# Second block scheme in a fused attention and tanh-shrink kernel: two groups of the first matrix, thirteen normalizations on ScalarE, one shared store of buffers

## The chip, the cores and the metric

The kernel runs on one core of one Trainium2 chip. The metric is the device time of one execution in microseconds, as the median of several runs. A profiled execution also gives a trace: what every engine did and when. The engines are TensorE (PE, with its weight loads as PEld), VectorE (DVE), ScalarE (ACT), GpSimd (POOL) and SyncE (SP); POOL, SP and ACT also issue DMAs from queues of their own, in order.

## The reference

Attention over 4 batches, 8 heads, 768 positions and 64 dimensions, where each query sees 96 local keys and 8 global ones, and then an MLP over the 3072 tokens of 512 features:

```python
scores = scale * np.matmul(q, k.transpose(0, 1, 3, 2)) + bias   # bias: -slope * distance
scores = np.where(is_global | is_local, scores, -1e9)
a = softmax(scores)
x = (a @ v) as 3072 x 512
h = x @ w_in            # 512 x 2048
g = h - np.tanh(h)
out = g @ w_out         # 2048 x 512
```

## The kernel before

**Tiles.** The 3072 tokens are 24 tiles of 128, numbered in the order in which they are worked on. Attention goes tile by tile: transposes of q and k (T, by PE for the first tiles and by DMA from SP's queue afterwards), scores on PE (S, line 375), exp on ACT (E, line 382), the mask as a product on DVE (M, line 386), the product with v on PE (AV, line 401; v has a column of ones, which yields the sum), and the normalization on DVE (R, lines 409 and 410: a reciprocal of 8 numbers a row, and a product that writes x, 512 columns). The 8 global rows of k and v are copied into each tile's own buffers (K and V, DVE copies). Then x is transposed (X and Xe for the first eight tiles, a DMA on SP's queue afterwards, Xe, line 432).

**First matrix.** Tiles are put in groups: groups 0 and 1 have one tile, 2 to 6 have two, 7 to 9 have four. W_in's 2048 columns are 16 blocks f of 128. For groups of four tiles an operation m1.g.f is four matmuls (line 443) of 128 x 128 weights over 512 columns (tokens) into one PSUM bank; th.g.f is the tanh on ACT from that bank (line 453), and g.g.f the subtraction on DVE (line 467), which writes g in bf16.

**Second matrix.** Each pair of tiles a, a+1 is multiplied with W_out by a block scheme with seven products instead of eight (Strassen's, in a form with intermediate sums): n1 to n4 are sums of blocks of g on DVE (line 507), w1 to w4 sums of blocks of W_out (line 494, once), p1 to p7 the products on PE (line 522), each of eight matmuls of 256 columns with its own weights. Some products accumulate onto one bank one after another, and what stands there is copied out between them (a0, a1, a2: 256 columns to SBUF, ACT or DVE, lines 253 and 255). c11, c12, c21 and c22 make the four blocks of the result (line 536 and the copy helper), and st stores 128 rows (line 539) from POOL's or SP's queue. For the last pair p3 and c12 are cut in halves.

**Order.** The list ORDER gives the order of issue on all engines at once, one word for each operation: `m1.8.11` is group 8, block 11; a side after a slash (`a1.14/a`) names the engine where there is a choice (a ACT, d DVE, p POOL, s SP). Each engine works through its own words in this order and waits only for what it needs. The list HOMES names the buffer or bank that each holder uses. Both lists are written out; the rest of the code only says what each word does. Buffers of three kinds (kq natural q and k, qk transposed q and k, pr exponentials) are separate sets of 5, 11 and 5 buffers, 2 KB a partition each.

Of the kernel before, what the change touches and what calls it, by code (L numbers as in the profile page):

```python
# [20 lines left out]
lq.4 Te.2.0/a AV.1 E.0.0 S.2 R.1 in.2 B.3 E.2.0 lk.4 AV.0 S.3 R.0 X.1 in.4 E.3.0 AV.2 Xe.1/d X.0 in.5 R.2 bm.2 Xe.0/a  # L21
AV.3 m1.1.0 lk.5 em.2 R.3 X.2 m1.0.0 th.1.0 Xe.2/d X.3 lq.5 th.0.0 g.1.0 m1.0.2 Xe.3/a g.0.0 m1.1.2 th.0.2 m1.2.2 th.1.2
g.0.2 g.1.2 lv.4 m1.2.6 th.2.2 lk.6 g.2.2 T.4.0 th.2.6 m1.2.0 Te.4.0/a m1.1.4 lq.6 th.2.0 m1.0.4 lv.5 th.1.4 g.1.4 T.4.1
m1.2.4 Te.4.1/a g.2.0 th.0.4 S.4 th.2.4 g.0.4 out.0 m1.2.10 E.4.0 K.4 g.2.6 m1.1.8 E.4.1 M.4.0 m1.2.8 g.2.4 th.1.8 out.1
M.4.1 th.2.10 m1.2.12 th.2.8 g.1.8 out.2 T.5.1 g.2.10 th.2.12 T.5.0 m1.1.12 out.3 Te.5.1/d Te.5.0/a g.2.12 S.5 lk.7
th.1.12 g.2.8 AV.4 g.1.12 E.5.1 lq.7 m1.0.8 R.4 E.5.0 m1.0.12 lq.10 M.5.1 M.5.0 T.6.1 lq.9 th.0.12 X.4 T.6.0 V.4 Xe.4/a
K.5 n1.0 AV.5 Te.6.1/a m1.2.14 R.5 th.0.8 Te.6.0/a lk.10 X.5 th.2.14 S.6 Xe.5/d g.0.12 m1.3.4 E.6.1 g.0.8 m1.3.6 g.2.14
lq.8 w1.0 m1.3.10 th.3.6 n3.0 th.3.4 m1.3.8 n2.0 E.6.0 w1.1 m1.3.12 th.3.10 g.3.6 lk.8 p1.0 g.3.4 m1.3.0 n1.2 a0.0/a
th.3.8 w3.0 m1.3.2 th.3.0 w2.0 lk.9 p2.0 w2.1 lv.6 w3.1 p6.0 g.3.0 T.7 lv.7 p7.0 n3.2 a1.0/a th.3.2 w4.0 p5.0 th.3.12
g.3.2 n2.2 a2.0/a p1.2 g.3.10 p2.2 a0.2/a c22.0 w4.1 p6.2 n4.2 T.8 p4.0 c11.0 a1.2/a g.3.12 p5.2 c21.0 T.9 M.6.1  # L30
st.1.0/p p7.2 a2.2/a c11.2 lv.8 g.3.8 T.10 p3.2 K.6 lq.13 V.5 M.6.0 S.7 c12.2/a c22.2 lq.11 AV.6 n4.0 E.7.1 p4.2 lk.12
R.6 E.7.0 m1.3.14 st.2.0/p M.7.1 lv.10 K.7 X.6 V.6 th.3.14 M.7.0 p3.0 Xe.6/a lv.9 c21.2 AV.7 g.3.14 c12.0/a lk.11 R.7
S.8 lq.12 n1.4 X.7 E.8.0 p1.4 Xe.7/d V.7 n2.4 m1.4.8 E.8.1 M.8.0 lk.13 m1.4.10 a0.4/a K.9 M.8.1 th.4.8 lk.15 p6.4 g.4.8
th.4.10 lv.11 E.9.0 g.4.10 m1.4.14 a1.4/d S.9 th.4.14 g.4.14 p5.4 E.10.1 K.10 M.9.0 m1.4.0 E.9.1 n3.4 T.11 AV.8 M.10.1
th.4.0 m1.4.4 a2.4/d E.10.0 T.12 R.8 p7.4 th.4.4 g.4.0 st.3.0/s m1.4.6 M.9.1 Xe.8 g.4.4 p2.4 th.4.6 c22.4 T.13 AV.9 n4.4
m1.4.12 R.9 m1.4.2 g.4.6 Xe.9 p3.4 c11.4 th.4.2 M.10.0 th.4.12 p4.4 g.4.2 c12.4/a g.4.12 st.4.0/p S.10 V.9 lq.14 n1.6
p1.6 E.11.1 c21.4 lq.15 n2.6 p2.6 E.11.0 a0.6/d lk.14 K.11 AV.10 c11.6 E.12.0 lv.12 p6.6 K.12 R.10 lq.16 m1.5.10 V.10
a1.6/a M.11.0 lk.16 S.11 th.5.10 lv.13 g.5.10 p5.6 E.12.1 M.11.1 m1.5.8 E.13.0 n4.6 T.14 AV.11 n3.6 th.5.8 m1.5.2 R.11
E.13.1 T.15 m1.5.12 g.5.8 th.5.2 M.12.1 m1.5.14 Xe.11 th.5.12 V.11 a2.6/a M.12.0 m1.5.0 M.13.0 Xe.10 AV.12 g.5.2 th.5.0
m1.5.6 th.5.14 R.12 T.16 p7.6 th.5.6 V.12 g.5.12 p3.6 Xe.12 c22.6 g.5.6 m1.5.4 c12.6/a g.5.14 st.6.0/p g.5.0 p4.6 th.5.4  # L40
lv.14 g.5.4 S.12 lv.15 M.13.1 p1.8 E.14.0 c21.6 st.5.0/p K.15 n1.8 m1.6.4 lk.18 E.15.0 K.14 a0.8/d AV.13 n2.8 lk.17
# [36 lines left out]
p.6.0:2 s.6.1:2,3 p.6.1:1 av.6:0,1 xt.6:7 x.6:0 s.7.0:4,5 p.7.0:1 s.7.1:6,7 p.7.1:3 av.7:4,5 xt.7:4 x.7:0 s.8.0:0,1
p.8.0:1 s.8.1:2,3 p.8.1:3 av.8:6,7 x.8:0 s.9.0:6,7 p.9.0:2 s.9.1:0,1 p.9.1:4 av.9:2,3 x.9:2 s.10.0:2,3 p.10.0:1
# [36 lines left out]
def kernel(  # L116
# [50 lines left out]
    u = 0  # L167
# [530 lines left out]
```

## Time and profile before

| | us |
|---|---|
| median of 3 runs | 204.03 (204.01 to 205.84) |
| the profiled execution | 203.72 |
| its span, first to last instruction | 202.0 |
| PE busy, 2147 matmuls | 194.3 |
| DVE busy, 360 instructions | 169.1 |
| ACT busy, 199 instructions | 120.0 |
| POOL busy, 102 instructions | 77.8 |

The span is what the trace covers; the execution's own time holds some 1.7 us more around it. In a row of instructions of the trace stand the start, the time, the engine, the line of the code, the operation, what it writes and reads with its shape, how many of them in a row, and in brackets how long the engine was idle before and which instruction ended that. A group's row ends with the total, the mean of one in ns, and the idle time of the engine before such instructions. Rows of one line give least, median and most of the duration in ns. Issues of DMAs are listed with their size and the median time from issue to landing.

### The profile page before, as it was taken

The page shows a single profiled execution, that of the slowest core. Times are in us where ns is not written, and L with a number is a line of the kernel's source. Part 1 is how long each engine was busy: PE and PEld are TensorE (multiplying, and loading weights), DVE is VectorE, ACT ScalarE, POOL GpSimd, SP SyncE. Part 2 cuts the span into 40 slices and gives each one's busy share as a digit, 9 for nine tenths or more (in the row PEclk, how much of TensorE's full clock was granted, in tenths as well). Part 3 has the DMA queues.
Part 4 walks back from the last instruction along what each step waited for, and adds up shares of the span by engine and source line. Part 5 has one row for each costly group of instructions (what it writes and reads, how often), then busy time and mean ns, then how long its engine had stood idle before and what let it go on. Part 6 is the DMA issues. An engine that isn't in the chain of part 4 may idle for free.

```text
span 202.0 us, 5299 instructions
## 1 busy us (share of the span) xinstructions
PE 194.3 (96%) x2147; PEld 149.8 (74%) x2147; DVE 169.1 (84%) x360; ACT 120.0 (59%) x199; POOL 77.8 (39%) x102
## 2 busy tenths in 40 slices
PE   7799999999999999999999999999999999999991
PEld 2469888888888988888988654787655456778890
DVE  6685798999998998999999799899896799659731
ACT  3798888652679287756746866686345563542120
POOL 8986485351981066069129900404001000001212
PEclk9999999999999999999999999999999999999999
DMA  5999999999999989979979999899250201002133
GB/s 142 218 184 184 194 167 207 198 154 151 204 172 156 206 132 134 167 159 169 142 155 160 185 127 167 161 92 148 67 130 0 104 3 52 0 0 109 52 124 136
DMA packets 103175, 27.33 MB, mean 135 GB/s; under 512 B 93920, under 2 KB 101344, under 8 KB 103152
## 3 DMA queue, kind: packets, MB, share of 16 engines
q0 software_dynamic: 74400, 17.90, 89.7%
q1 hardware_dynamic: 28208, 8.59, 25.2%
q10 hardware_dynamic: 544, 0.52, 1.0%
q8 instruction: 16, 0.26, 0.5%
q14 instruction: 7, 0.06, 0.1%
HBM read 27.26 MB, written 6.29 MB: 166 GB/s over the span
## 4 chain that ended last, share of the span: by engine, by line
PE 54%; issue 15%; DMA 12%; POOL 8%; DVE 8%; POOLq 0%
PE ps L443 28%; PE ps L522 19%; DMA w_out_bf<-in_moe_w_out_dram 6%; DMA w_in_bf<-in_moe_w_in_dram 6%; PE ps L401 4%; PE ps L375 4%; POOL w_in_bf L324 2%; POOL vb L321 2%; DVE gall L467 2%; POOL out_dram L539 2%; POOL kq L318 1%; DVE wc L494 1%; DVE pr L386 1%; DVE ot L536 1%; POOL kq L321 1%
## 5 line engine op out<-in xcount | busy, mean ns | idle before, releaser
L443 PE MATMUL ps<-xT,w_in_bf 128*128 128x256 bf16 (+2 forms) x640 | 91.1, 294 | 0.0
L467 DVE TENSOR_TENSOR gall<-ps,th 128x512 bf16<-128x512 f32 (+1 forms) x98 | 63.0, 673 | 14.9 <-ACT th L453 14.4
L453 ACT ACTIVATE th<-ps 128x512 f32<-128x512 f32 (+1 forms) x98 | 55.4, 591 | 32.6 <-PE ps L443 30.2
L443 PEld LDWEIGHTS <-w_in_bf 128*128 128x128 bf16 x640 | 56.4, 98 | 22.6
L522 PEld LDWEIGHTS <-gall 128*128 128x128 bf16 x488 | 46.6, 98 | 8.1 <-issue 0.5
L539 POOL DMA_DIRECT2D out_dram<-ot x19 | 10.8, 567 | 106.4 <-ACT ot L253 40.3
L382 ACT ACTIVATE pr<-ps 128x1024 bf16<-128x1024 f32 x44 | 43.5, 1025 | 6.2 <-PE ps L375 3.6
L522 PE MATMUL ps<-w_out_bf,gall 128*128 128x256 bf16 (+1 forms) x296 | 36.7, 270 | 0.4 <-DVE ot L255 0.4
L386 DVE TENSOR_TENSOR pr<-pr,mk 128x1024 bf16<-128x1024 bf16 x40 | 26.7, 680 | 0.6 <-ACT pr L382 0.5
L253 ACT COPY sn<-ps 128x256 f32<-128x256 f32 x29 | 10.8, 371 | 27.1 <-PE ps L522 27.0
L522 PE MATMUL ps<-f,ss 128*128 128x256 bf16 x192 | 24.9, 273 | 0.0
L522 PE MATMUL ps<-wc,gall 128*128 128x256 bf16 x192 | 24.9, 273 | 0.0
L321 POOL DMA_DIRECT2D vb<-in_v_dram x24 | 21.5, 906 | 1.2 <-DMA w_in_bf<-in_moe_w_in_dram 0.7
L321 POOL DMA_DIRECT2D kq<-in_k_dram x20 | 18.1, 912 | 6.3 <-DMA w_out_bf<-in_moe_w_out_dram 4.4
L522 PEld LDWEIGHTS <-ss 128*128 128x128 bf16 x192 | 18.1, 98 | 2.9
L536 DVE TENSOR_TENSOR ot<-ps,sn 128x256 f32<-128x256 f32 x36 | 14.8, 418 | 5.6 <-PE ps L522 4.3
L321 POOL DMA_DIRECT2D kq<-in_q_dram x20 | 18.0, 911 | 3.4 <-DMA w_out_bf<-in_moe_w_out_dram 2.0
L410 DVE TENSOR_TENSOR x<-ps,rden 128x512 bf16<-128x512 f32 x24 | 16.6, 692 | 1.1 <-DVE rden L409 0.3
L401 PEld LDWEIGHTS <-pr 128*128 128x128 bf16 x352 | 13.4, 97 | 2.6 <-ACT pr L382 0.5
L401 PE MATMUL ps<-vb,pr 128*128 128x65 bf16 x352 | 14.8, 193 | 0.0
L375 PEld LDWEIGHTS <-qk 64*128 64x128 bf16 x352 | 10.0, 94 | 3.5 <-issue 2.7
L375 PE MATMUL ps<-qk 64*128 64x128 bf16 x192 | 9.4, 218 | 0.0
(57 smaller groups left out, 122.9 us busy)
## 6 DMA issues: line engine op xcount, KB each, us to landing
out_dram<-ot POOLq DMA_DIRECT2D x18, 256.0 KB, 2.5
vb<-in_v_dram POOLq DMA_DIRECT2D x24, 128.0 KB, 5.8
kq<-in_q_dram POOLq DMA_DIRECT2D x22, 128.0 KB, 6.8
kq<-in_k_dram POOLq DMA_DIRECT2D x22, 128.0 KB, 6.7
w_out_bf<-in_moe_w_out_dram POOLq DMA_DIRECT2D x4, 512.0 KB, 10.8
out_dram<-ot SPq DMA_DIRECT2D x5, 256.0 KB, 2.5
w_in_bf<-in_moe_w_in_dram POOLq DMA_DIRECT2D x4, 256.0 KB, 7.4
w_in_bf<-in_moe_w_in_dram POOLq DMA_DIRECT2D x2, 512.0 KB, 11.2
```

The costliest lines, as they stand in the source:

```text
L321: eng(e).dma_start(out=dst, in_=rows_of(src, u).rearrange("h p d -> p h d"))
L375: nc.tensor.matmul(bank(("s", u, o), hh)[:, p * P : (p + 1) * P], buf(("qk", back[u] if o else u))[r, 1, p, :], buf(("qk", u))[r, 0, p, :] ...
L382: nc.scalar.activation(d, banks(("s", u, o), 0, 1), AF.Exp, bias=0.0, scale=scale)
L386: nc.vector.tensor_tensor(out=t, in0=t, in1=mk[:, mask_of(u, o)], op=ALU.mult)
L401: nc.tensor.matmul(t[:, h // (H // 2), h % (H // 2), :], buf(("p", u, o))[:, slot(h), :], buf(("v", back[u] if o else u))[:, h, 0 : Dh + 1 ...
L410: nc.vector.tensor_tensor(out=buf(("x", u)).rearrange("q (a h) d -> q a h d", a=2), in0=t[:, :, :, 0:Dh], in1=rden.to_broadcast([P, 2, H / ...
L443: nc.tensor.matmul(t[:, (f - f0) * n : (f - f0 + 1) * n], w_in_bf[j][:, c, fo : fo + P], x[:, c, 0:n], start=(c == 0), stop=(c == CD - 1),)
L453: nc.scalar.activation(h_view(buf(("th", g, f0)), g, m), h_view(bank(("h", g, f0)), g, m), AF.Tanh, bias=0.0, scale=1.0)
L467: nc.vector.tensor_tensor(out=o, in0=v(h), in1=v(th), op=ALU.subtract)
L522: nc.tensor.matmul(bank((holder, a))[:, c0:c1], s(f), t(f)[:, c0:c1], start=first and f == 0, stop=f == HF - 1, skip_group_check=not first,)
L536: nc.vector.tensor_tensor(out=o, in0=bank((holder, a))[:, 0:DH2], in1=buf(("sn", a, k)), op=ALU.add)
L539: eng(e).dma_start(out=out[turn_of[u] * P : (turn_of[u] + 1) * P, c0:c1], in_=buf(("ot", u))[:, c0:c1])
```

## The change

**The first matrix of groups 8 and 9 by a block scheme.** W_in's 16 blocks of columns are four runs of four blocks. For runs j = 1, 2, 3 of groups 8 and 9 (six units g.j) the sixteen m1 matmuls of 512 columns are replaced by seven products d1 to d7, each of four matmuls of 256 columns (two blocks of outputs r, two of the contraction c). Run 0 keeps m1. A unit has three banks: r and q (side by side in the code as `qr`) and z. d1 starts r, and e0 copies its 512 columns to SBUF in fp32 (k0); d6 accumulates onto r, e1 copies; d5 accumulates, e2 copies; d3 accumulates, and r then holds one block of h. d2 goes to q, and q11 (DVE) adds k0 to it. d7 goes to z, q22 adds it to e2's copy; d4 accumulates onto z, q21 adds it to e1's copy. The tanh and the subtraction are as many as before, 512 columns each, but read their h from two banks or two SBUF buffers. y1 to y4 are four sums of x blocks for each of the two groups, v1 to v4 four sums of W_in blocks for each of the three runs, on DVE, 512 bf16 columns each.

```diff
+    DUNITS = [(8, 1), (8, 2), (8, 3), (9, 1), (9, 2), (9, 3)]
...
+    def wi_sum(j, k):
+        a, b = 4 * j, 4 * j + 2
+        x, y, o = {
+            1: (w_in_two(b, 0), w_in_two(b, 2), ALU.add), 2: (wsum(j, 1), w_in_two(a, 0), ALU.subtract),
+            3: (w_in_two(a, 0), w_in_two(b, 0), ALU.subtract), 4: (w_in_two(a, 2), wsum(j, 2), ALU.subtract),
+        }[k]
+        nc.vector.tensor_tensor(out=wsum(j, k), in0=x, in1=y, op=o)
+
+    def x_sum(g, k):
+        b11, b12, b21, b22 = (x_block(g, i, j) for i in (1, 2) for j in (1, 2))
+        x, y = {1: (b12, b11), 2: (b22, xsum(g, 1)), 3: (b22, b12), 4: (b21, xsum(g, 2))}[k]
+        nc.vector.tensor_tensor(out=xsum(g, k), in0=x, in1=y, op=ALU.subtract)
...
+    def in_product(g, j, k):
+        a, b = 4 * j, 4 * j + 2
+        part, w, x, first = {
+            1: ("r", lambda r: w_in_of(a + r, 0), x_block(g, 1, 1), True),
+            2: ("q", lambda r: w_in_of(a + r, 2), x_block(g, 2, 1), True),
+            3: ("r", lambda r: wsum(j, 4)[:, :, r * P : (r + 1) * P], x_block(g, 2, 2), False),
+            4: ("z", lambda r: w_in_of(b + r, 2), xsum(g, 4), False),
+            5: ("r", lambda r: wsum(j, 1)[:, :, r * P : (r + 1) * P], xsum(g, 1), False),
+            6: ("r", lambda r: wsum(j, 2)[:, :, r * P : (r + 1) * P], xsum(g, 2), False),
+            7: ("z", lambda r: wsum(j, 3)[:, :, r * P : (r + 1) * P], xsum(g, 3), True),
+        }[k]
+        t = d_bank(g, j, part)
+        for r in range(2):
+            for c in range(2):
+                nc.tensor.matmul(
+                    t[:, r * 2 * P : (r + 1) * 2 * P], w(r)[:, c], x[:, c], start=first and r + c == 0, stop=c == 1,
+                    skip_group_check=not first or r > 0,
+                )
+
+    def d_copy(e, g, j, k):
+        copy(e, d_keep(g, j, k), d_bank(g, j, "r"))
+
+    def d_add(g, j, k):
+        if k == 0:
+            q = d_bank(g, j, "q")
+            nc.vector.tensor_tensor(out=q, in0=q, in1=d_keep(g, j, 0), op=ALU.add)
+            return
+        a = d_keep(g, j, k)
+        nc.vector.tensor_tensor(out=a, in0=d_bank(g, j, "z"), in1=a, op=ALU.add)
```

**Normalization.** R keeps only the reciprocal; the product is a word of its own, N, with a choice of engine. Eleven tiles have it on DVE as before (N/d), thirteen on ACT (N/a: 4, 8, 9, 11 to 15, 17, 20 to 23), where it is eight activations of 64 columns, one a head, whose scale is a column of the reciprocals.

```diff
+    def a_N(e, u):
+        t, rden = av(u), rdens[home(("rd", u))[0]]
+        if e is ACT:
+            for h in range(H):
+                a, b = divmod(h, H // 2)
+                nc.scalar.activation(
+                    buf(("x", u))[:, h, :], t[:, a, b, 0:Dh], AF.Copy, bias=0.0, scale=rden[:, a, b, :]
+                )
+            return
```

**K and V.** They get a choice of engine: 8 of 16 K and 7 of 16 V go to ACT.

**One store.** The 21 buffers of kq, qk and pr become slots of one tile `mem` of the same total size; the new sums and copies (ws, xs, k0, k12: one or two slots each) take slots of it too, and HOMES says who has which.

```diff
-    buffers("kq", NK, [P, 2, H * Dh], BF16)
-    buffers("qk", NQK, [P, 2, NP, P], BF16)
+    mem = pool.tile([P, NM, 2 * H * Dh], BF16, name="mem")
...
-    buffers("pr", 5, [P, H, P], BF16)
```

**Order and homes.** Both lists are new from the normalization of the first tiles on. Stores go from SP's queue twelve times instead of seven and from POOL's fourteen instead of nineteen. The new list where the block products are, and its end:

```diff
+p3.12 M.22.0 E.22.1 S.18 c22.12 M.21.0 c12.12/a p4.12 E.23.0 M.20.1 st.12.0/p p1.14 M.21.1 lv.23 E.23.1 M.23.0 AV.20
+st.11.0/p y1.8 d1.8.1 V.20/a y2.8 d2.8.1 R.20 e0.8.1/a y4.8 AV.21 N.20/a c21.12 d6.8.1 M.22.1 m1.8.0 a0.14/a R.21 Xe.20
+q11.8.1 e1.8.1/a p2.14 N.21/a n3.14 V.21/d d5.8.1 c11.14 th.8.0 Xe.21 d1.8.3 y3.8 e2.8.1/a g.8.0 AV.22 e0.8.3/a d3.8.1
+R.22 M.23.1 d7.8.1 N.22/a p6.14 V.22/d q22.8.1 th.8.5 Xe.22 d1.8.2 n4.14 th.8.4 d4.8.1 e0.8.2/a g.8.5 d6.8.3 q21.8.1
+d2.8.2 e1.8.3/a d6.8.2 g.8.4 th.8.6 d5.8.3 q11.8.2 e1.8.2/a AV.23 e2.8.3/a g.8.6 d7.8.3 a1.14/a d2.8.3 R.23 th.8.7
+q22.8.3 d5.8.2 N.23/a d3.8.3 q11.8.3 d4.8.3 g.8.7 e2.8.2/a Xe.23 d7.8.2 th.8.13 q21.8.3 d3.8.2 th.8.12 p5.14 q22.8.2
...
+p5.18 g.9.11 th.9.1 c21.16 p7.18 g.9.6 a2.18/a st.17.0/s th.9.10 g.9.0 p3.16 g.9.1 p3.18 g.9.10 c22.18 p1.20 n1.20 p2.20
...
+st.22.0/p p5.22 p3.20 a2.22/d c22.22 p3.22.0 c11.20 c12.20/a p4.22 st.20.0/s c12.22.0/a st.22.256/p p3.22.1 c21.22
+c12.22.1/a st.23.0/s st.22.384/s
```

More of the change, by code (lines that the diff above doesn't have):

```diff
@@ L25 @@
[L25 to L29, printed above, removed]
@@ new lines @@
+q21.8.2 d1.9.1 g.8.15 th.8.10 d2.9.1 g.8.14 e0.9.1/a m1.8.2 th.8.11 g.8.1 th.8.3 m1.9.3 y2.9 a2.14/a q11.9.1 p3.14
+g.8.10 th.9.3 g.8.3 d6.9.1 th.8.2 m1.9.2 g.8.11 e1.9.1/a c12.14/a y3.9 d5.9.1 g.9.3 th.9.2 st.14.0/p d1.9.2 e2.9.1/a
+y4.9 d2.9.2 g.8.2 e0.9.2/a d7.9.1 c22.14 d3.9.1 q22.9.1 d6.9.2 th.9.5 n1.16 p1.16 th.9.4 g.9.5 e1.9.2/a p4.14 q11.9.2
+a0.16/a d4.9.1 g.9.4 d5.9.2 q21.9.1 d1.9.3 e2.9.2/a n3.16 d2.9.3 e0.9.3/a d7.9.2 c21.14 n2.16 d3.9.2 st.15.0/s d6.9.3
+n1.18 p6.16 e1.9.3/a q22.9.2 d5.9.3 n3.18 a1.16/a d7.9.3 e2.9.3/a g.9.2 d4.9.2 th.9.9 p5.16 q22.9.3 th.9.7 q11.9.3
@@ L112 @@
+ot.16:2 ot.17:2 r.18:5 q.18:7 z.18:3 sn.18.0:2 sn.18.1:1 sn.18.2:0 ss.18.1:2 ss.18.2:1 ot.18:3 ot.19:0 r.20:2 q.20:4
+z.20:7 sn.20.0:0 sn.20.1:2 sn.20.2:1 ss.20.1:2 ss.20.2:1 ot.20:0 ot.21:1 r.22:3 q.22:5 z.22:7 sn.22.0:1 sn.22.1:3
+sn.22.2:1 ss.22.1:0 ss.22.2:3 ot.22:3 ot.23:1 g.0:0 g.2:1 g.4:2 g.6:0 g.8:2 g.10:0 g.12:1 g.14:2 g.16:0 g.18:1 g.20:3
+g.22:4 mk.1:2,3 mk.2:0,1 f32.0.k:3 f32.0.q:2 f32.1.k:1 f32.1.q:0
 """
@@ L221, in home, with mems @@
         return homes[".".join(map(str, holder))]
-    KIND = {"v": "vb", "p": "pr"}
-    def buf(holder):
+    KIND = {"v": "vb"}
+    def mems(holder, dt):
+        i, j = home(holder)
+        t = mem[:, i : j + 1, :].rearrange("q a f -> q (a f)")
+        return t if dt is BF16 else t.bitcast(dt)
+    def buf(holder):
+        k = holder[0]
+        if k in ("kq", "qk", "p", "k0"):
+            t = mem[:, home(holder)[0], :]
+            if k == "kq":
+                return t.rearrange("q (a f) -> q a f", a=2)
+            if k == "qk":
+                return t.rearrange("q (a p f) -> q a p f", a=2, p=NP)
+            return t.rearrange("q (h f) -> q h f", h=H) if k == "p" else t.bitcast(FP32)
         return bufs[KIND.get(holder[0], holder[0])][home(holder)[0]]
@@ L446, in m1, with w_in_of, w_in_two, four @@
                 )
+    def w_in_of(f, c):
+        j = in_of[f]
+        return w_in_bf[j][:, c : c + 2, (f - in_from[j]) * P : (f - in_from[j] + 1) * P]
+    def w_in_two(f, c):
+        j = in_of[f]
+        fo = (f - in_from[j]) * P
+        return w_in_bf[j][:, c : c + 2, fo : fo + 2 * P]
+    def four(holder):
+        return mems(holder, BF16).rearrange("q (k c f) -> q k c f", k=4, c=2)
+    def wsum(j, k):
+        return four(("ws", j))[:, k - 1]
+    def xsum(g, k):
+        return four(("xs", g))[:, k - 1]
@@ new lines, in d_bank, with d_keep @@
+    def d_bank(g, j, part):
+        return bank(("zd", g, j)) if part == "z" else bank(("qr", g, j), 0 if part == "q" else 1)
+    def d_keep(g, j, k):
+        return buf(("k0", g, j)) if k == 0 else mems(("k12", g, j), FP32)[:, (k - 1) * 4 * P : k * 4 * P]
+    def in_product(g, j, k):
[16 more added lines that the diff above has]
+                )
@@ L448, in h_view, with d_th, d_g @@
+    def d_th(g, f):
+        o = buf(("th", g, f)).rearrange("q (b n) -> q b n", b=2)
+        nc.scalar.activation(o, h_of(g, f), AF.Tanh, bias=0.0, scale=1.0)
+    def d_g(g, f):
+        us = groups[g]
+        i, j = home(pair_of(us[0]))[0], home(pair_of(us[2]))[0]
+        th = buf(("th", g, f)).rearrange("q (b n) -> q b n", b=2)
+        nc.vector.tensor_tensor(out=gall[:, i : j + 1 : j - i, f, :], in0=h_of(g, f), in1=th, op=ALU.subtract)
     def h_view(t, g, m):
@@ L598 @@
         if 1 <= nth[u] < NQ - 1:
-            op(("K", u), DVE, lambda e, u=u: a_K(e, u))
-            op(("V", u), DVE, lambda e, u=u: a_V(e, u))
+            op(("K", u), None, lambda e, u=u: a_K(e, u))
+            op(("V", u), None, lambda e, u=u: a_V(e, u))
         op(("AV", u), PE, lambda e, u=u: a_AV(u))
         op(("R", u), DVE, lambda e, u=u: a_R(u))
+        op(("N", u), None, lambda e, u=u: a_N(e, u))
         if u < PE_X:
@@ L613 @@
         for f, m in ([(0, 2), (2, 2)] if m == 4 else []) + [(f, m) for f in range(4 if m == 4 else 0, CF, m)]:
+            if (g, f // 4) in DUNITS:
+                op(("th", g, f), ACT, lambda e, g=g, f=f: d_th(g, f))
+                op(("g", g, f), DVE, lambda e, g=g, f=f: d_g(g, f))
+                continue
             op(("m1", g, f), PE, lambda e, g=g, f=f, m=m: m1(g, f, m))
@@ L616 @@
             op(("g", g, f), DVE, lambda e, g=g, f=f, m=m: m1_g(g, f, m))
+    for j in sorted({j for _, j in DUNITS}):
+        for k in range(1, 5):
+            op((f"v{k}", j), DVE, lambda e, j=j, k=k: wi_sum(j, k))
+    for g in sorted({g for g, _ in DUNITS}):
+        for k in range(1, 5):
+            op((f"y{k}", g), DVE, lambda e, g=g, k=k: x_sum(g, k))
+    for g, j in DUNITS:
+        for k in range(1, 8):
+            op((f"d{k}", g, j), PE, lambda e, g=g, j=j, k=k: in_product(g, j, k))
+        for k in range(3):
+            op((f"e{k}", g, j), None, lambda e, g=g, j=j, k=k: d_copy(e, g, j, k))
+        for w, k in (("q11", 0), ("q21", 1), ("q22", 2)):
+            op((w, g, j), DVE, lambda e, g=g, j=j, k=k: d_add(g, j, k))
     for x in range(2):
```

179 lines of the change are left out of this document (91 added, 88 removed).

## The prediction

> **What bounds the kernel now.** I read the page's top lines, then the table of stretches, then the chain that ended last.
>
> ```profile
> span 202.0 us, 5299 instructions
> PE 194.3 (96%) x2147; PEld 149.8 (74%) x2147; DVE 169.1 (84%) x360; ACT 120.0 (59%) x199; POOL 77.8 (39%) x102
> ```
> ```profile
> 140.00:150.00 10.00, 10.00 (x86) 5.79 (x83) 8.86 (x19) 5.43 (x10) 0.00 (x0) 1.00 0.62 110
> 150.00:160.00 10.00, 10.00 (x56) 5.34 (x55) 6.68 (x13) 4.71 (x9) 1.14 (x2) 1.00 0.20 66
> 160.00:170.00 10.00, 10.00 (x59) 5.51 (x58) 9.53 (x16) 5.06 (x10) 0.54 (x1) 1.00 0.07 28
> 170.00:180.00 10.00, 10.00 (x75) 7.05 (x73) 6.50 (x12) 5.05 (x11) 0.00 (x0) 1.00 0.00 0
> 180.00:190.00 10.00, 10.00 (x94) 8.96 (x92) 8.24 (x17) 2.26 (x6) 1.08 (x2) 1.00 0.15 55
> ```
> ```profile
> 116.12 0.48 PE ps L401 x16
> 116.61 4.32 PE ps L443 x20
> ...
> 154.90 9.50 PE ps L443 x44
> ```
>
> The columns of the table are the stretch, its length, and then PE, PEld, DVE, ACT and POOL busy, each with its count. PE fills every stretch, at a granted clock of 1.00. The busy column alone would not prove that (a pipelined matmul also counts while it drains), but the chain does: long runs of matmuls follow each other there with no wait between. PE is the bound, and time is matmul columns. In the same stretches DVE has 0.5 to 3.5 us free in each ten, ACT five or more: this is where the change spends.
>
> **1. The block scheme, groups 8 and 9, runs 1 to 3: six units.** Before, a unit is 16 matmuls of 512 columns; after, 28 of 256. The first kind costs 9.50/44 = 0.216 us each (4.32/20 gives the same). The second kind is what line 522 issues:
>
> ```profile
> 195.59 1.04 PE L522 MATMUL ps<-wc,gall 128*128 128x256 bf16 x8
> 196.46 0.61 PE L522 MATMUL ps<-w_out_bf,gall 128*128 128x128 bf16 x8
> 197.45 0.61 PE L522 MATMUL ps<-w_out_bf,gall 128*128 128x128 bf16 x8 [0.38 <-DVE ot L255]
> ```
> ```profile
> L443 PEld LDWEIGHTS <-w_in_bf 128*128 128x128 bf16 x640 | 56.4, 98 | 22.6
> ```
>
> Eight of them start at 195.59 and the next run at 196.46: 0.109 us each (the 1.04 holds 0.17 of drain). So 16 x 0.216 = 3.46 becomes 28 x 0.109 = 3.05, and six units save 6 x 0.41 = 2.4 us. Twelve more weight loads a unit lie under the matmuls: 98 ns against 109. Without that cover they would add 12 x 0.098 = 1.2 us a unit. The bounds are thus -2.4 and, with no cover, +4.7; I take -2.4, because line 522 already runs this very pattern, one load to each 256 columns, at 0.109.
>
> The Trainium skill (TensorE: Matmul & The Clock Gate, section Back-to-back issue gap) gives for streams of loads and matmuls about 131 ns a matmul at 512 columns and 81 at 128. By that rule, as an estimate, a unit would go from 16 x 131 = 2.1 us to at least 28 x 81 = 2.3, and the change would lose 1 us or more. The trace disagrees: 216 ns at 512 and 109 at 256, exactly the ratio of the columns.
>
> **2. What the scheme gives to ACT and DVE.** Each unit needs three copies of 512 fp32 from PSUM on ACT (e0, e1, e2) and three additions of 512 on DVE (q11, q21, q22); beside these stand 12 sums of weights and 8 of x (512 bf16 each).
>
> ```profile
> 159.88 3.08 DVE L467 TENSOR_TENSOR gall<-ps,th 128x512 bf16<-128x512 f32 x5 [0.44 <-ACT th L453]
> ...
> 187.03 0.75 DVE L536 TENSOR_TENSOR ot<-ps,sn 128x256 f32<-128x256 f32 x2
> 187.70 0.68 DVE L507 TENSOR_TENSOR gall<-gall,ss 128x1024 bf16<-128x1024 bf16 x1
> ```
> ```profile
> DVE gall L467 <- ACT th L453: 8.1, 10, 1.4
> ```
> ```profile
> L410 DVE TENSOR_TENSOR x<-ps,rden 128x512 bf16<-128x512 f32 x24 | 16.6, 692 | 1.1 <-DVE rden L409 0.3
> L409 DVE RECIPROCAL rden<-ps 128x8 f32<-128x8 f32 x24 | 4.8, 198 | 1.2 <-PE ps L401 0.9
> ```
>
> Five of line 467 in 3.08 with 0.68 for one: in a row one takes 0.60. Of 256 columns one takes 0.75 - 0.42 = 0.33 in a row, and 1024 bf16 take 0.6 to 0.68. So the additions cost 18 x 0.60 = 10.8. The 20 sums are bounded by 0.30 (half of line 507) and 0.68; I take 0.33, as they have half its elements: 6.6 us. Thirteen normalizations leave (13 x 0.69 = 9.0).
>
> I count the list from y1.8 to the last g of group 9. PE has 42 block products (18.3), 8 m1 (8 x 4 x 0.216 = 6.9), 19 second-matrix products (19 x 8 x 0.109 = 16.6) and three AV (1.5): 43.3. DVE has 32 g (19.2), 18 additions (10.8), 10 g sums (6.0), 8 x sums (2.6), 6 results (2.0), two masks (1.3) and small ones (0.8): 42.7. The margin is 0.6 us. Before, this engine could wait for tanh 8.1 us between 144 and 182 (the wait row), at no cost. I expect most of those waits to go, for DVE now runs behind its inputs; some 1.2 us may stay, of which the margin absorbs half. The x sums take the full transposed x of a group, the last part of which is asked for some 4.8 us of PE work ahead:
>
> ```profile
> xT<-x SPq DMA_TRANSPOSE x16, 2.6
> ```
>
> so the transposes stay hidden unless a normalization is over 2 us late.
>
> **3. Thirteen normalizations on ACT: eight 64-column activations each, with a scale per partition.** No such instruction is in the trace.
>
> ```profile
> L253 ACT COPY sn<-ps x29: 367/372/374, 40.2 to 194.0; 128x256 f32<-128x256 f32 x29
> L253 ACT CAST qk<-ps x3: 585/586/592, 7.6 to 10.3; 128x512 bf16<-128x512 f32 x3
> L253 ACT COPY xT<-ps x4: 580/582/585, 13.9 to 55.0; 128x512 bf16<-128x512 bf16 x4
> ```
> ```profile
> 144.07 0.37 ACT L253 COPY sn<-ps 128x256 f32<-128x256 f32 x1
> 144.32 0.62 ACT L453 ACTIVATE th<-ps 128x512 f32<-128x512 f32 x1
> ```
> ```profile
> 148.88 1.08 ACT L453 ACTIVATE th<-ps 128x512 f32<-128x512 f32 x2 [0.74 <-PE ps L443]
> ```
>
> From 256 to 512 columns a copy grows 0.586 - 0.372 = 0.214, so 64 would last 0.21 alone; in a row 0.12 of it overlaps (a 0.37 copy is followed after 0.25, and two tanh take 1.08: 0.49 each). So eight cost from 8 x 0.09 = 0.7 us to, if narrow ones are no cheaper than the 256-wide copy, 8 x 0.25 = 2.0. I take 1.0: near the low end, since the three widths lie on one line, with something for the scale.
>
> What does that price decide? Take the first unit of group 8. PE accumulates d6, d5 and d3 onto one bank, and each must wait until ACT has copied out what was there. From the end of d1.8.1 to d3.8.1 the list gives PE two block products, AV.21, m1.8.0, p2.14, two more block products and AV.22: 4 x 0.437 + 2 x 0.485 + 0.864 + 0.873 = 4.45 us. In that time ACT must do e0, N.20, a0.14, e1, N.21, th.8.0 and e2. Without the two N that is 3 x 0.49 + 0.25 + 0.49 = 2.2, and 0.1 for the first, which overlaps nothing: 2.3; drain and semaphores take 0.25 more (0.17 of drain above, and line 522 restarts 0.05 after the copy that held it). So each N may take 0.95 us. At 1.0 PE waits 0.1; at 2.0 it waits 2.1. Before d6.8.2 ACT has e0.8.3, N.22, two tanh and e0.8.2, with room for 1.4; between d5.8.2 and d3.8.2 stands N.23, with room for some 1.1. A single copy of 512 with its drain and semaphores needs 0.85, and the closest pairs of products (d6 and d5 of 8.3, 9.1 and 9.3) are 0.87 apart: enough, with nothing over.
>
> The Trainium skill (ScalarE: Activation LUTs, section What ACT_TABLE_LOAD costs) speaks against this part. It gives 186 ns + 0.833 ns a column for an activation with immediate operands, about 93 ns more for each per-partition pointer, and 93 ns of overlap. As an estimate from that page, 64 columns with a pointer are 186 + 53 + 93 - 93 = 239 ns, or 1.9 us a tile, and the sum below would end near 204.5 instead of 201.5. The trace agrees with the first part (613 by the page, 586 to 600 measured); no run here shows a pointer.
>
> **4. Small parts.** Eight K and seven V copies move to ACT:
>
> ```profile
> L255 DVE COPY qk<-qk x16: 148/169/530, 23.5 to 134.5; 128x32 bf16<-128x32 bf16 x16
> L255 DVE COPY vb<-vb x16: 269/279/779, 31.7 to 144.9; 8x512 bf16<-8x512 bf16 x16
> ```
>
> There a V lasts about 0.58 (as the 512-wide copy), a K between 0.15 (DVE's own) and 0.37; most stand in stages where ACT has room. The shared store changes which slot a load waits for, not how many bytes move: zero, with the list issuing loads 5 us or more ahead of their transposes as before. If that cover went, a transpose's 2.6 us would show. Five stores go from POOL's queue to SP's, where the x transposes queue behind them. At the end, p4.22 now stands between the halves of p3.22 and fills the 0.38 us that PE waits at 197.45, while st.23 (256 KB, 2.5 us to landing, against 1.8 for the 64 KB one that ends the kernel before) leaves a little later: -0.4 to +0.3, taken as -0.3.
>
> ```profile
> out_dram<-ot SPq DMA_DIRECT2D x5, 256.0 KB, 2.5
> out_dram<-ot POOLq DMA_DIRECT2D x1, 64.0 KB, 1.8
> ```
>
> **Sum.** The profiled execution took 203.7 us (span 202.0), 0.3 below the median of the runs, 204.03. 203.7 - 2.4 (columns) - 0.3 (tail) + 0.5 (DVE waits that reach PE, and 0.1 from N) = 201.5 us.
>
> **Rivals.**
> A, forecast: PE stays the bound. 201.5, by itself 200.6 to 202.4.
> B, narrow activations are dear. At 1.5 to 2.0 us an N, the bank of unit 8.1 holds PE for 1.1 to 2.1 us, N.22 and N.23 for 0.5 to 1.5 more, and the back-to-back N.8 and N.9 for up to 1. On top of 201.5 that is 203 to 206, around 204. For it: nothing in the trace is as small. Against: the straight line of widths.
> C, DVE becomes the bound and it is slower than before. Place: the 43.3 us of the block stage. If the 8.1 us of waits for tanh recur, DVE needs 42.7 + 8.1 = 50.8 us there, PE waits 7.5, and the time is 203.7 - 2.7 + 7.5 = 208.5. It decides from 3.3 us of waits on. Against: those waits came when DVE had nothing else queued.
> D, the halved matmuls do not run at half the time; at 0.123 us each (28 x 0.123 = 3.46) nothing is saved: 203.9. Against: 0.109 on line 522.
>
> **How the numbers follow.** A 0.55, B 0.28, C 0.12, D 0.05. About 1%, or 2 us, is what a measurement here tells from no change. Faster by over 1% (under 202.0): nearly nine tenths of A, 0.48. Slower by over 1% (over 206.1): C and the top of B, 0.14. The rest, 0.38. The range reaches from 200.5 (A with no DVE wait and the tail's best) to 205.2, which leaves out C and the dearest of B.
>
> **What would show it.** Right: block products at 0.109 a matmul, line 443 at 0.216, no wait of PE over 0.3 us between y1.8 and the last g, an N on ACT near 1 us, DVE at 95% or more in that stage. An N of 1.5 us or more, with block products waiting for ACT copies, shows B; PE waiting for line 467 shows C. The forecast is wrong if PE's idle time after its first 60 us exceeds 1.5 us.

## The result and the profile after

The changed kernel takes 211.6 us (median of six runs) against 204.5 for the kernel before in the same runs: a ratio of 1.032, 95% interval 1.027 to 1.037. It is slower. The forecast was 201.5 us, in a range of 200.5 to 205.2. A few executions fall into a slower state with a lower granted clock; the medians and ratios of all runs here leave those out.

The top of the page of the changed kernel's profiled execution (211.69 us):

```profile
span 209.9 us, 5660 instructions
PE 196.0 (93%) x2219; PEld 157.8 (75%) x2219; DVE 176.6 (84%) x375; ACT 151.2 (72%) x331; POOL 75.0 (36%) x97
```

The table of stretches of the same execution, columns as before (start and end, length, then busy time and count of PE, PEld, DVE, ACT and POOL, then the granted clock):

```profile
60.00:110.00 50.00, 48.83 (x631) 42.53 (x628) 44.29 (x95) 43.10 (x107) 20.97 (x26) 1.00 1.53 148
110.00:130.00 20.00, 17.30 (x151) 10.18 (x149) 14.32 (x28) 12.58 (x21) 11.67 (x14) 0.91 1.79 163
130.00:145.00 15.00, 14.58 (x176) 10.73 (x173) 14.02 (x30) 12.68 (x27) 0.44 (x1) 1.00 0.67 99
145.00:165.00 20.00, 17.85 (x193) 14.27 (x191) 17.16 (x36) 19.07 (x58) 1.58 (x3) 1.00 0.44 86
165.00:185.00 20.00, 19.96 (x167) 16.05 (x165) 19.65 (x37) 13.85 (x29) 0.56 (x1) 1.00 0.08 28
```

The same stretches of the kernel before:

```profile
60.00:110.00 50.00, 50.00 (x658) 43.85 (x657) 46.89 (x100) 32.66 (x49) 22.23 (x28) 1.00 1.49 158
110.00:130.00 20.00, 20.00 (x178) 11.51 (x176) 18.06 (x35) 14.23 (x23) 7.57 (x10) 1.00 1.58 165
130.00:145.00 15.00, 15.00 (x196) 11.66 (x195) 14.17 (x32) 9.68 (x14) 2.90 (x4) 1.00 0.98 108
145.00:165.00 20.00, 20.00 (x123) 10.71 (x121) 15.50 (x28) 11.35 (x21) 1.14 (x2) 1.00 0.21 60
```

PE filled every stretch before. Now it lacks 1.2, 2.7, 0.4 and 2.2 us in the first four, and the clock is down in the second. In the fourth, ACT is full (19.07 of 20) and DVE is not: the late engine there is ACT. In the last row PE is full again, with DVE at 98%.

What PE waited for, the longest of the list of waits:

```profile
PE ps L397 <- DMA mem<-mem: 2.7, 1, 2.7
PE ps L532 <- ACT x L436: 1.3, 2, 1.1
...
PE ps L532 <- ACT mem L275: 0.7, 1, 0.7
```

The first is a transpose of q and k by DMA that came late (line 397 is the scores); the others are block products (line 532) held by ScalarE. This is the row of ScalarE's normalization, line 436:

```profile
L436 ACT ACTIVATE x<-ps,rden 128x64 bf16<-128x64 f32 x104 | 22.5, 334 | 1.7 <-DVE rden L429 1.7
```

One lasts 334 ns by its record, not the 208 of the straight line. In a row, eight of them and what follows:

```profile
147.40 1.70 ACT L436 ACTIVATE x<-ps,rden 128x64 bf16<-128x64 f32 x8
148.98 0.38 ACT L275 COPY sn<-ps 128x256 f32<-128x256 f32 x1
```

The next instruction starts 1.58 us after the first of the eight: 0.198 us each, 1.6 us a tile where the prediction took 1.0.

### The profile page after: what moved, and what is told of

The parts are those of the page before. It is cut to its first block, busy times and chain, and to the rows that moved or that the text cites. A ratio compares the mean times of both kernels' runs of the same rounds, so it can differ in the third digit from the quotient of the medians.

```text
span 209.9 us, 5660 instructions
## 1 busy us (share of the span) xinstructions
PE 196.0 (93%) x2219; PEld 157.8 (75%) x2219; DVE 176.6 (84%) x375; ACT 151.2 (72%) x331; POOL 75.0 (36%) x97
## 4 chain that ended last, share of the span: by engine, by line
PE 57%; ACT 17%; DMA 12%; DVE 7%; issue 4%; POOL 1%; DVEq 0%; ACTq 0%; POOLq 0%
PE ps L639 28%; PE ps L473 16%; ACT x L436 9%; PE ps L532 6%; DMA mem<-in_q_dram 6%; PE ps L397 4%; DMA mem<-mem 4%; ACT th L570 3%; DMA mem<-in_k_dram 3%; ACT mem L275 2%; DVE mem L408 2%; DVE gall L584 2%; PE ps L423 2%; ACT mem L404 1%; POOL mem L340 1%
## 5 line engine op out<-in xcount | busy, mean ns | idle before, releaser
L473 PE MATMUL ps<-xT,w_in_bf 128*128 128x256 bf16 (+2 forms) x544 | 69.7, 279 | 0.1
L584 DVE TENSOR_TENSOR gall<-ps,th 128x512 bf16<-128x512 f32 (+1 forms) x74 | 47.7, 667 | 11.2 <-ACT th L570 10.8
L404 ACT ACTIVATE mem<-ps 128x1024 bf16<-128x1024 f32 x44 | 43.2, 1026 | 2.9 <-PE ps L397 2.7
L408 DVE TENSOR_TENSOR mem<-mem,mk 128x1024 bf16<-128x1024 bf16 x40 | 26.9, 680 | 3.6 <-ACT mem L404 3.2
L436 ACT ACTIVATE x<-ps,rden 128x64 bf16<-128x64 f32 x104 | 22.5, 334 | 1.7 <-DVE rden L429 1.7
L343 POOL DMA_DIRECT2D mem<-in_q_dram x20 | 17.8, 895 | 6.3 <-DMA w_out_bf<-in_moe_w_out_dram 2.7
L343 POOL DMA_DIRECT2D mem<-in_k_dram x20 | 18.1, 908 | 5.4 <-DMA mem<-mem 2.8
L397 PE MATMUL ps<-mem 64*128 64x128 bf16 x352 | 14.3, 221 | 3.9 <-DMA mem<-mem 2.7
L275 ACT COPY mem<-ps 128x512 f32<-128x512 f32 (+1 forms) x23 | 13.5, 606 | 3.2 <-PE ps L532 2.3
L423 PEld LDWEIGHTS <-mem 128*128 128x128 bf16 x352 | 13.3, 97 | 2.9 <-issue 0.5
```

Source lines behind the costliest of these rows:

```text
L275: nc.scalar.copy(out=out, in_=in_)
L343: eng(e).dma_start(out=dst, in_=rows_of(src, u).rearrange("h p d -> p h d"))
L397: nc.tensor.matmul(bank(("s", u, o), hh)[:, p * P : (p + 1) * P], buf(("qk", back[u] if o else u))[r, 1, p, :], buf(("qk", u))[r, 0, p, :] ...
L404: nc.scalar.activation(d, banks(("s", u, o), 0, 1), AF.Exp, bias=0.0, scale=scale)
L408: nc.vector.tensor_tensor(out=t, in0=t, in1=mk[:, mask_of(u, o)], op=ALU.mult)
L423: nc.tensor.matmul(t[:, h // (H // 2), h % (H // 2), :], buf(("p", u, o))[:, slot(h), :], buf(("v", back[u] if o else u))[:, h, 0 : Dh + 1 ...
```

## The experiments

Theory N: the price of the narrow activations makes ScalarE late, and the rest follows from it. Theory S: the new order and the shared store lose the time by themselves, through tight banks, late loads or VectorE. In the table the ratio is that to the kernel before, measured alongside, with its 95% interval. n_wide, n_imm and n_imm_eighth leave out all or most of the normalization of the thirteen tiles; they are probes, not remedies.

| run | us, median | ratio |
|---|---|---|
| the change | 211.6 | 1.032 (1.027 to 1.037) |
| n_wide | 202.7 | 0.988 (0.981 to 0.994) |
| n_imm | 202.9 | 0.990 (0.985 to 0.995) |
| n_dve | 205.7 | 1.005 (1.003 to 1.008) |
| before_n_act | 215.2 | 1.051 (1.046 to 1.056) |
| n_1315_dve | 207.5 | 1.014 (1.008 to 1.019) |
| n_2023_dve | 208.9 | 1.022 (1.013 to 1.030) |
| n_dve_copies_act | 205.6 | 1.002 (0.999 to 1.006) |
| n_pool | 205.5 | 1.003 (0.998 to 1.007) |
| n_imm_eighth | 205.2 | 1.001 (0.998 to 1.004) |
| mix_pool | 204.4 | 0.999 (0.996 to 1.002) |
| mix_pool_late | 204.7 | 1.000 (0.998 to 1.003) |

**n_wide: one activation instead of eight.**

```diff
-            for h in range(H):
-                a, b = divmod(h, H // 2)
-                nc.scalar.activation(
-                    buf(("x", u))[:, h, :], t[:, a, b, 0:Dh], AF.Copy, bias=0.0, scale=rden[:, a, b, :]
-                )
+            nc.scalar.activation(
+                buf(("x", u)).rearrange("q (a h) d -> q a h d", a=2), t[:, :, :, 0:Dh], AF.Copy, bias=0.0, scale=rden[:, 0, 0, :]
+            )
```

> The changed kernel, with the normalization on ScalarE as one activation over all 512 columns instead of eight of 64 (all heads take the first head's reciprocal, so the normalization of seven heads in eight is left out for the thirteen tiles). Theory N (the price of the eight narrow activations, about 1.6 us a tile in a row instead of the 1.0 of the prediction, makes ScalarE late, and everything else follows): one takes 0.6 to 0.75 us, the wait of TensorE for the transposed q and k near 115 us goes, TensorE's waits for ScalarE in the block stage go, 201 to 203.5 us. Rival S (the new order and the shared store lose the time by themselves, by tight banks, late loads or VectorE): 207 us or more.

Measured: 202.7 us. Its row of the normalization:

```profile
L434 ACT ACTIVATE x<-ps,rden 128x512 bf16<-128x512 f32 x13 | 8.8, 684 | 1.8 <-DVE rden L429 1.7
```

The same order, store and block scheme, 8.9 us less. Theory S falls.

**n_imm: eight activations, without the pointer** (`scale=1.0` instead of `scale=rden[:, a, b, :]`).

> The changed kernel, with the eight 64-column activations a tile kept, but with the immediate scale 1.0 instead of the column of reciprocals (the normalization of the thirteen tiles is left out). If the pointer is what makes them dear: mean some 0.21 to 0.24 us instead of 0.33, eight in a row in 0.8 to 1.0 us, and 202 to 204 us. If it is their number, the mean stays near 0.3 us, eight take 1.5 us or more and the time stays at 209 to 212 us. Rival S: 207 us or more with any price.

Measured: 202.9 us. Its row, and eight in a row with what follows:

```profile
L436 ACT ACTIVATE x<-ps 128x64 bf16<-128x64 f32 x104 | 13.3, 265 | 1.7 <-DVE rden L429 1.7
```
```profile
100.99 1.04 ACT L436 ACTIVATE x<-ps 128x64 bf16<-128x64 f32 x8 [0.71 <-DVE rden L429]
101.83 1.24 ACT L570 ACTIVATE th<-ps 128x512 f32<-128x512 f32 x2
```

A slot of 0.84 us for eight, 0.105 each, as expected; the mean by the records, 265 ns, lies above the 210 to 240 that were expected. So neither their number and width alone made them dear, nor the pointer alone, which n_wide's single instruction also has: the pointer to a scale per partition in each of eight instructions did, by 0.093 us an instruction in a row, 0.74 us a tile, 9.7 us of ScalarE over thirteen tiles. The straight line of widths gave 0.09 and was nearly right for what it described. The Trainium skill (ScalarE: Activation LUTs, section What ACT_TABLE_LOAD costs) states about 93 ns for each pointer operand. The spacing in a row agrees with that (0.093 us); the lengths of the records differ by less, 334 - 265 = 69 ns. The prediction's estimate of the whole instruction by that page, 239 ns, is 41 ns above the 198 measured in a row.

**n_dve: all normalizations on VectorE** (each `N.u/a` in the list becomes `N.u/d`).

> The changed kernel, with all 24 normalizations on VectorE at the same places of the order. Theory N: ScalarE is on time again; VectorE gets 13 x 0.63 = 8.2 us more, 2.5 of them in the block stage, where its margin was worked out as 0.6 us, so TensorE waits some 2 to 3 us there: 203 to 205.5 us. Rival S: 207 us or more.

Measured: 205.7 us, just above what was expected. The stretch of the block stage:

```profile
145.00:165.00 20.00, 19.08 (x176) 14.87 (x175) 20.00 (x39) 14.55 (x29) 0.00 (x0) 1.00 0.21 54
```

Now DVE has no free time at all, and PE waits 0.9 us, less than the 2 to 3 that were expected. With the normalizations on VectorE what the scheme saves is lost again: 205.7 us against 202.9 in n_imm.

**before_n_act: the thirteen normalizations on ScalarE, in the kernel before.**

```diff
-... R.11 ...
+... R.11 N.11/a ...
```

> The kernel before with one part of the change alone: the same thirteen normalizations on ScalarE, at the place in the order that they had on VectorE. ScalarE is 59% busy there, and the order was not drawn up for it. Theory N: each takes 1.6 us instead of 0.65 and holds up what stands behind it on ScalarE (exponentials, tanh) and the transposes of x: 205 to 208 us, with TensorE waiting where the transposes of q and k queue behind a late transpose of x. Rival S: ScalarE has room, VectorE gets 9 us free: 203.5 to 205 us.

Measured: 215.2 us, outside both. The direction is theory N's; the size is not. With no block scheme at all, one part of the change alone costs 10 us in an order that was not drawn up for it. What PE waited for there, of the list of waits:

```profile
PE ps L451 <- ACT pr L382: 1.8, 2, 1.3
...
PE ps L401 <- ACT pr L382: 1.7, 1, 1.7
...
PE ps L335 <- ACT pr L382: 0.5, 1, 0.5
```

These waits are for the exponentials (pr, line 382), 4.0 us in sum. The two pages account for the span's 11.7 us (213.7 against 202.0): PE is idle for 8.3 us more, and its same 2147 matmuls count 3.4 us more as busy. Of the 8.3, 2.5 more are waits for VectorE's subtraction (line 475), whose own waits for tanh rise from 14.4 to 29.9 us. So ScalarE's lateness reaches PE through VectorE too; the rest was not followed.

**n_1315_dve and n_2023_dve: where the change loses it.** Only tiles 13 to 15, or only 20 to 23, go back to VectorE.

> The changed kernel with the normalizations of tiles 13, 14 and 15 back on VectorE; the other ten stay on ScalarE. Theory N, place one: these three hold back the DMA transposes of x on SyncE's queue, behind which the transpose of tile 19's q and k waits, for which TensorE waits 2.7 us at 114.9 and after which its granted clock is below 1.00 for a while (0.91 on average from 110 to 130). With them on VectorE that wait and the clock loss should go: 206.5 to 208.5 us, the block stage as late as before. If the wait is rather made by the bunch of loads that GpSimd issues from 109.7 on, it stays and the time stays at 209.5 to 212.

> The changed kernel with the normalizations of tiles 20 to 23 back on VectorE; the other nine stay on ScalarE. Theory N, place two: in the block stage TensorE's waits for ScalarE go (2.2 us of idle time between 145 and 165), but VectorE gets 4 x 0.63 = 2.5 us in a stage with a margin of 0.6, so most is given back: 209 to 211.5 us, the wait at 114.9 unchanged.

Measured: 207.5 and 208.9 us. The first is as theory N had it. The second is just below its range, and its runs lie so far apart (208.4 to 211.2) that its comparison with the kernel before is unclear. The first place is a queue. This is SyncE's queue in the changed kernel, then what PE did with it:

```profile
104.92 4.89 SPq L462 DMA_TRANSPOSE xT<-x  x3
110.00 7.84 SPq L378 DMA_TRANSPOSE mem<-mem  x2
```
```profile
114.49 0.40 PE L397 MATMUL ps<-mem 64*128 64x128 bf16 x8
117.59 1.03 PE L397 MATMUL ps<-mem 64*128 64x128 bf16 x16 [2.70 <-DMA mem<-mem]
```

Before the three transposes of x (Xe.14, Xe.13, Xe.15) the queue waits for ScalarE twice, 2.6 and 1.1 us; behind them stands T.19, whose loads were issued by 98.1 and took some 5 us. It is issued at 110.00 and lands 7.5 us later; PE waits 2.7 us. In n_1315_dve it is issued at 108.00 and lands after 3.9 us, and no wait of PE for a transpose is left between 100 and 130:

```profile
108.00 8.70 SPq L378 DMA_TRANSPOSE mem<-mem  x2
```

So T.19 lands 5.6 us earlier, of which the queue makes 2.0 and the transfer itself 3.6. What differs for the transfer is GpSimd's bunch of loads, which starts at 109.69 in the change, 0.3 us before T.19, and at 109.32 in n_1315_dve, 1.3 us after it. In n_dve and mix_pool T.19 also leads the loads by 1.3 us and takes 3.9 and 4.0 us; in n_pool and n_2023_dve it follows them and takes 6.2 and 7.8. With a lead of 0.8 us it takes 5.1 (n_wide), with 0.4 us 6.8 (n_imm); in the kernel before, with 0.6 us, only 4.0. The loads, which the expectation named as the other explanation, thus seem to be part of the wait: late normalizations push the transpose behind them. No run moved the loads alone.

After the wait in the changed kernel the clock is low:

```profile
116.00:117.00 1.00, 0.00 (x0) 0.00 (x0) 0.85 (x2) 0.00 (x0) 0.97 (x2) 1.00 2.35 156
117.00:118.00 1.00, 0.41 (x10) 0.42 (x12) 0.00 (x0) 0.00 (x0) 0.79 (x2) 0.56 2.43 155
118.00:119.00 1.00, 1.00 (x15) 0.68 (x12) 0.00 (x0) 0.55 (x2) 1.00 (x2) 0.50 2.43 155
119.00:120.00 1.00, 1.00 (x6) 0.72 (x5) 0.28 (x1) 1.00 (x2) 1.00 (x2) 0.50 2.43 155
120.00:121.00 1.00, 1.00 (x6) 0.50 (x4) 1.00 (x2) 1.00 (x2) 0.89 (x2) 0.73 2.41 156
```

The eighth column is the granted clock: some 3.4 us at half speed, a loss of 1.7 us that no wait shows. Not every execution has it: four of the change's six runs have a mean granted clock of 0.99 and take 211.5 to 211.9 us, the other two have 1.00 and take 209.7 and 210.2. Nor does the length of the wait decide it: in n_2023_dve PE waits 3.0 us for the same transpose, and the clock stays at 1.00, while a wait of 1.9 us at 6.6 to 8.5 us is followed by 0.50. So n_1315_dve gained 4.1 us against the median of the change, and 2.4 against the two runs without the clock loss, where the wait was worth 2.7 in the trace.

The second place is the block stage, where PE's waits for ScalarE stood in the list above. In n_2023_dve PE's idle time from 145 to 165 falls from 2.2 to 0.8 us, with VectorE full (19.96 of 20), and 0.6 us appears from 165 to 185. Its two runs at a clock of 1.00 (208.4 and 208.9) are 1.3 us below the change's two.

**n_imm_eighth: one product more in each unit.** In n_imm, the block product d7 is issued twice.

> The run with eight activations of immediate scale (the normalization of the thirteen tiles left out), in which the seventh product of each of the six units is issued twice, the second time over the first. That gives TensorE 24 matmuls of 256 columns more, 24 x 0.109 = 2.6 us, and nothing to any other engine: as much as the block scheme is to save. If TensorE is the bound in that stage: 2.0 to 3.0 us more than the run without it. If VectorE or the round trips through ScalarE set the pace there, the products disappear in waits that are there anyway: under 1 us more.

Measured: 205.2 us against 202.9, 2.4 more, where 24 matmuls last 2.6; by the two ratios it is 2.2, give or take 1.2. From 145 to 165 PE is busy for all 20.00 us, and VectorE's 19.93 fall to 18.56. TensorE is the bound of the block stage when ScalarE is on time, and a product saved there counts nearly in full.

**Three ways to keep the scheme.** n_dve_copies_act moves all normalizations to VectorE and 27 plain copies to ScalarE. n_pool lets ScalarE copy (no pointer) and GpSimd multiply:

```diff
+            xb = buf(("x", u)).rearrange("q (a h) d -> q a h d", a=2)
+            nc.scalar.activation(xb, t[:, :, :, 0:Dh], AF.Copy, bias=0.0, scale=1.0)
+            nc.gpsimd.tensor_tensor(out=xb, in0=xb, in1=rden.to_broadcast([P, 2, H // 2, Dh]), op=ALU.mult)
```

mix_pool is n_pool with tiles 13 to 15 on VectorE, mix_pool_late with tiles 4, 8, 9 and 11 to 15 there.

> The changed kernel with all normalizations on VectorE, and in exchange every plain copy that the list gives to VectorE for the second matrix and for the global rows (8 keeps, 2 results, 8 K, 9 V) on ScalarE, where no pointer is needed. VectorE then has about as much work as in the changed kernel, without the dear activations: 202.5 to 204.5 us by theory N, against 205.7 with the normalizations moved alone. It ends above 205 if the block stage alone, where few copies are there to move, sets the time.

> The changed kernel with the thirteen normalizations split: ScalarE copies the 512 columns out of PSUM in one activation with an immediate scale, and GpSimd multiplies them in place by the reciprocals. ScalarE is as in the one-activation run; GpSimd's product should take 1 to 1.5 us, so a transpose of x starts about as late as with eight activations, but ScalarE itself is on time. If the lateness of ScalarE is what costs most (theory N): 202.5 to 205.5 us, with some wait left at the transpose of tile 19. If the late x itself costs most: 207 us or more.

> The changed kernel with the normalizations of tiles 13 to 15 on VectorE and those of the other ten split between ScalarE (a copy) and GpSimd (the product, 1.12 us). It joins the two remedies: nothing dear on ScalarE, and the transposes of x of tiles 13 to 15 early enough that tile 19's transpose lands in time. Theory N: 203 to 204.5 us. If GpSimd's longer way to the transposes costs as much as the pointers did, 205 us or more.

> As the run before, but with GpSimd's product only for tiles 17 and 20 to 23; tiles 4, 8, 9, 11 to 15 are normalized on VectorE. GpSimd is spared where it issues most loads, VectorE gets up to 8 x 0.63 = 5.0 us more before 110 us, where it has some 0.5 us in ten free: 203 to 205 us. Faster than the run before if GpSimd's products delayed loads there, slower if VectorE is the tighter of the two.

Measured: 205.6, 205.5, 204.4 and 204.7 us. The first missed, and the reason that its expectation named is only part of it: in the block stage DVE is full (20.00 of 20) and PE idle for 0.7 us, but PE is idle for 1.5 us from 130 to 145 as well. The second ends at the top of its range. The two mixtures came as expected. None of the four can be told from the kernel before. GpSimd's product takes 1117 ns. The block stage of n_pool:

```profile
145.00:165.00 20.00, 19.39 (x179) 15.32 (x180) 20.00 (x39) 16.45 (x33) 4.15 (x4) 1.00 0.21 55
```

The same stretch of n_imm:

```profile
145.00:165.00 20.00, 19.98 (x181) 15.83 (x178) 19.93 (x38) 17.73 (x48) 0.57 (x1) 1.00 0.22 61
```

VectorE is full in both, but PE lacks 0.6 us in n_pool. Part of that shows in the trace: while GpSimd's product runs from 144.72 to 145.93, a copy of global rows of v on VectorE (8 x 512, line 277), begun at 144.96, takes 1.12 us, and the next one, at 147.94, takes 0.28; a sum of g, begun at 148.75 under the next product, takes 1.01 us, where such sums take 0.69 in n_imm. Whether the longer way to the x sums adds to that was not tried.

## Why the prediction was wrong

**The step that failed is step 3**: "I take 1.0: near the low end, since the three widths lie on one line, with something for the scale." The line was right, 0.105 us a narrow activation; the scale costs as much again, 0.093, or 0.74 us a tile where the prediction had put 0.3 beside the 0.7 of its line. So N takes 1.6 us, not 1.0, and the sum's 0.1 us from N became 2.0 us of waits in the block stage alone. Rival B had the mechanism, with 0.28, at 203 to 206 us.

**B's price was too small as well, and its mechanism only partly right.** In the block stage its size fits: 2.0 us of waits, where B had 1.6 to 3.6. But only one of the three waits is of the kind that step 3 worked out:

```profile
151.54 0.60 PE L532 MATMUL ps<-xT,w_in_bf 128*128 128x256 bf16 x4 [1.05 <-ACT x L436]
154.70 0.60 PE L532 MATMUL ps<-xT,w_in_bf 128*128 128x256 bf16 x4 [0.29 <-ACT x L436]
161.59 0.60 PE L532 MATMUL ps<-xT,mem 128*128 128x256 bf16 x4 [0.70 <-ACT mem L275]
```

The last, d3.8.2, waits for a copy behind N.23, as B had it. The first two, d1.8.3 and d1.8.2, wait for N.21 and N.22 themselves: HOMES gives these units' r and q the very banks that AV.21 and AV.22 wrote (4 and 5, 2 and 3), and they come free when the normalization has read them. The prediction looked at the copies of a unit, not at who held its banks before.

What B missed was the queue. Step 2 said that the transposes "stay hidden unless a normalization is over 2 us late", and looked only at the transposes of x. The transpose of tile 19's q and k stands behind them; that cost 2.7 us and, in four runs of six, 1.7 by the clock. The new list was enough to see the order: it has T.19 after Xe.14, Xe.13 and Xe.15.

**Step 1, the saving: right.** From the chain of the changed kernel:

```profile
166.97 1.73 PE ps L473 x8
...
170.87 2.62 PE ps L532 x24
```

0.216 and 0.109 us. With N cheap the time is 202.7 to 202.9; a product more in each unit costs 2.4. Rival D falls. The Trainium skill's 131 ns at 512 columns (TensorE: Matmul & The Clock Gate, Back-to-back issue gap) is not seen in these traces either.

**Step 2, VectorE: right.** It was put at 42.7 of 43.3 us, and runs at 98% (19.65 of 20) with PE full beside it. No wait of PE for VectorE stands between 144 and 185, in the change or in n_imm, so the 0.5 us set aside for that was not needed. C falls: VectorE's waits for tanh in that stage went from 8.1 to 2.4 us in the change and to 0.2 in n_imm, as the prediction held. But n_dve shows how little margin there was.

**Step 4: right in what it names.** The last half product follows the quarters without a wait, and the copies cost what was said, a V 0.60 us (the first row) and a K 0.23:

```profile
L275 ACT COPY vb<-vb 8x512 bf16<-8x512 bf16 x7 | 4.2, 604 | 0.3 <-PE ps L423 0.3
L275 ACT COPY mem<-mem 128x32 bf16<-128x32 bf16 x8 | 1.8, 226 | 3.9 <-PE ps L397 3.9
```
```profile
204.69 1.04 PE L639 MATMUL ps<-wc,gall 128*128 128x256 bf16 x8
205.56 0.61 PE L639 MATMUL ps<-w_out_bf,gall 128*128 128x128 bf16 x8
```

The step named 5 us of cover for the loads ahead of their transposes; what came late at 115 us was not the load but the issue of the transpose, which no term priced.

**What is left open.** The change is 8.8 us longer than n_imm by span (209.9 against 201.1). From 60 to 165 us PE is idle for 6.4 us (1.2, 2.7, 0.4 and 2.2), in n_imm for 1.2, which is 5.3 of the difference; in the first 60 us it is idle for 0.8 more. The other 2.7 lie in the busy column (196.0 against 193.3 for the same 2219 matmuls): the clock took 1.7 of them, and about 1 us is not placed; it may lie in waits shorter than the drain of a matmul, which that column hides. And n_imm is 1.4 us above the forecast. Half of that is the level of the comparison: the kernel before took 204.75 us (median) beside it, 0.7 above the 204.03 that the forecast started from. Tile 19's transpose still comes late there, by 1.1 us:

```profile
113.53 0.62 PE L397 MATMUL ps<-mem 64*128 64x128 bf16 x16 [1.13 <-DMA mem<-mem]
```

## What to carry to other kernels

Before moving work to an engine, price the exact form of the instruction: operands that no row of the trace has can cost as much as the work itself, and where the schedule's margin is smaller than that uncertainty, the uncertainty is the forecast. When an operation may become later, list everything that stands behind its consumers in their queues, not only who reads its result, and who takes over the banks that it reads. A page of the Trainium skill that states the price of just that operand deserves more than a rival's chance when the trace agrees with the rest of its formula.

## What the runs showed of the hardware

- A [128,1] pointer as scale adds 0.093 us to each activation in a row (0.198 against 0.105 us at 64 columns); by the lengths of the records it is 0.069 us.
- The granted clock fell to 0.50 for some 3.4 us after a wait of TensorE of 2.7 us (the change) and after one of 1.9 us (n_2023_dve). After waits of 3.0 us (n_2023_dve) and 1.1 us (n_imm) it stayed at 1.00.
- The same DMA transpose lands after 3.9 to 4.0 us when it is issued 1.3 us ahead of a bunch of loads, and after 6.2 to 7.8 us when it is issued 0.2 to 0.3 us behind their start.
- GpSimd multiplies 128 x 512 bf16 by a broadcast fp32 in 1.12 us; instructions of VectorE under it took 1.12 instead of 0.28 us and 1.01 instead of 0.69.
- 256-column matmuls with a weight load each run at 0.109 us whether the weights are W_in itself or sums of it.
